# Where the first folds run, and a start written out by hand, in a Fourier-transform and expert kernel

## The chip, the core and the metric

The kernel runs on one NeuronCore of a Trainium2 chip: TensorE (PE) multiplies matrices, VectorE (DVE), ScalarE (ACT) and GpSimd (POOL) work elementwise, SyncE (SP) issues most DMAs, and POOL issues those whose addresses come from data. The metric is the device time of one execution in microseconds, as the median of repeated runs.

## The reference

```python
X = np.fft.fft(x, axis=1)          # x: 8 batches, 2496 positions, 256 features, f32
X = np.fft.fft(X, axis=2)
x = X.real.reshape(19968, 256)     # tokens
logits = x @ w_gate                # 8 experts
e_idx = np.argmax(logits, axis=1)
gate_w = softmax(logits)[e_idx]
eom = 1.0 / (1.0 + np.exp(-(x @ w_output_gate)))
for e in range(8):
    mask = e_idx == e
    h = np.maximum(x[mask] @ w1[e], 0.0)        # 256 -> 1024
    out[mask] = gate_w[mask] * eom[mask, e] * (h @ w2[e])
```

## The kernel before

**Stages.** A batch of the transform is loaded as five tiles `xt` of 128 features by 8 groups of 128 positions (512 KB each), written (batch, chunk) below. For each tile `fold1` adds the two halves (one instruction on 500 or 512 elements per partition; from batch `LB` = 3 on, two more on 250 or 256), and `fold2` forms sums and differences in two to four more instructions and stores them in `ft`. Then `dstage` multiplies by the table of the first transform on PE (f32), `devac` takes the result out of PSUM as two f16 parts `ahi` (ACT) and `alo` (DVE), scaled by a power of two that `energy`, `energy_sum` and `scale` work out of the batch's energy; `sstage` multiplies by the tables of the second transform (`tst0`, `tstm`, `tstr`, `tstq`), and `sevac` makes rows of tokens. There are five S stages a batch, so 40 steps `n` = 5 b + i. `gating(b)` picks the expert of each token and a place in the scratch `scr`, and 20 scatters a batch, indirect DMAs of POOL (L653), write the rows there.

**The experts.** After step `FSTART` = 15 the expert loop begins: `load_x_` reads rows of one expert back from `scr` by a transposing DMA (L1075), after the table `slots_a` says where they lie, and `mm1` and `mm2` (L1115, L1135) run on them. The first table needs the rows of batches 0 and 1, that is their 40 scatters. The other steps of the transform are woven into the expert loop.

**Order.** SP and POOL run in the order in which the program text issues (`PH1`), under `manual_schedule(engines=PH1)`. The order on PE, DVE and ACT is chosen by a planner from its own simulated times. `steps()` issues step by step: the D stages of the next batch, the S stage of this one, the folds of tiles further ahead (`fc` counts them; `AHEAD` bounds how far), the evacuation, pieces of the gating with five scatters each, and the squares of the expert weights on ACT (`wsquare`, L367), for which `wload` issues two 1 MB loads ahead. Seven buffers hold `xt` tiles; `load_x` issues the next load on SP when a fold is through with a tile. PSUM holds three results of D or S stages.

**Lines that the change touches.** `fold1` (L413, L416, L417): its engine is handed over by the caller; in `start` it alternates between DVE and POOL, in `steps` (L978) it is POOL except for chunk 1 of batches below 3. `fold2` (L429, L432): on POOL for chunks 2 and 4 of batches 0 and 1, else on DVE; L441 and L443 are always on DVE. `start` (L932 to L955) issues batch 0; on SP it issues the loads of all seven `xt` buffers first, and `tst0` after all folds of batch 0.

Of the kernel before, what the change touches and what calls it, by code (L numbers as in the profile page):

```python
# [19 lines left out]
KC = 5  # L20
# [210 lines left out]
def fft_moe_kernel(ctx: ExitStack, tc: tile.TileContext, xl, wg, w1, w2, tde, tdo, gt, ts0, tsm, tsr, tsq, cst, tid, out):  # L231
    nc = tc.nc
# [43 lines left out]
    if True:  # L276
# [45 lines left out]
        load_x()  # L322
# [96 lines left out]
        def fold2(b, c):  # L419
# [4 lines left out]
            W = slice(0, KW[c])  # L424
            ft = f[c] = pf.tile([128, 2, 2, 128], F32, name="ft", tag="ft", bufs=7)
            h = int(b >= LB)
            v = xts[b, c].rearrange("p (h a b) n -> p h a b n", h=2, a=2)[:, h]
            eng = nc.gpsimd if b < 2 and c in (2, 4) else nc.vector
            eng.tensor_sub(ft[:, :, 1, W], v[:, :, 0, W], v[:, :, 1, W])  # L429
            yield  # L430
            e = v[:, :, 0]
            eng.tensor_add(e[:, :, W], e[:, :, W], v[:, :, 1, W])  # L432
# [499 lines left out]
        def start():  # L932
            gt_ = gate_tables()
            next(gt_)
            for c in range(KC):
                fold1(0, c, nc.gpsimd if c % 2 else nc.vector)
                if c == 2:
                    for _ in gt_:
                        pass
                weave(fold2(0, c))  # L940
                if c > 2:
                    dstage(0, c - 3)
            for j in range(2):
                load_t(j)
            nc.sync.dma_start(tidt, tid)
            for k in range(2):
                nc.sync.dma_start(scr[DUM + 128 * k:DUM + 128 * (k + 1), :], ztile)
            energy(0)
            energy_sum(0)
            scale(0)  # L950
            smalls.clear()
            for c in range(KC):
                if c > 1:
                    dstage(0, c)
                devac(0, c)  # L955

        def steps():
            wk = 0
            fc = KC
            for n in range(5 * NB):  # L960
# [11 lines left out]
                for j in range(2, 6) if n == 0 else ():  # L972
                    load_t(j)
                while fc <= min(KC * (b + 1) + AHEAD[b >= BA][i], KC + 3 * n + 2):
                    m = fc
                    fc += 1
                    if m < NB * KC:
                        fold1(*divmod(m, KC), nc.vector if m % KC == 1 and m // KC < 3 else nc.gpsimd)  # L978
                    if m - 1 < NB * KC and m > KC:
                        fillers.append(fold2(*divmod(m - 1, KC)))  # L980
                        if n < 2:
                            weave(fillers.pop())
# [246 lines left out]

    with tc.manual_schedule(engines=PH1):  # L1230
        start()
# [62 lines left out]
```

## Time and profile before

| | us |
|---|---|
| median of the runs shown | 1174.66 |
| the runs | 1174.36, 1174.66, 2767.52 |
| profiled execution, whole | 1159.36 |
| its span, first to last instruction | 1157.5 |

The profiled execution is 15.3 us shorter than the median. A time in the trace counts from the span's start. In a row of the timeline stand the start, the duration, the engine, the line, the operation, what it writes and reads, how many instructions are merged, and in brackets the idle time before it with what ended it. "SPq" is an issue on SP's queue.

### The profile page before, as it was taken

What the parts mean: (1) busy time and instruction counts of PE and PEld (TensorE: products, weight loads), DVE (VectorE), ACT (ScalarE), POOL (GpSimd) and SP (SyncE); (2) the same over time, 40 slices, a digit from 0 to 9 for tenths busy, and PEclk for the clock granted to TensorE, in tenths of its full rate; (3) what the DMA queues carried; (4) which work ended last, traced back from release to release, by engine and by line L of the source; (5) the groups of instructions that cost most, each with busy time, mean ns of one, the idle gap of its engine ahead of it and who ended that gap; (6) DMA issues with size and microseconds to landing.
All of it is one profiled execution on the core that took longest, in us unless ns stands there. A gap on an engine that the chain in (4) does not pass through costs nothing.

```text
span 1157.5 us, 28573 instructions
## 1 busy us (share of the span) xinstructions
PE 1052.7 (91%) x10060; PEld 934.4 (81%) x10060; DVE 833.0 (72%) x1535; ACT 731.6 (63%) x1216; POOL 498.6 (43%) x430
## 2 busy tenths in 40 slices
PE   3877469989999999998999999999999989999998
PEld 3666458878788887887878888889989979998887
DVE  7876797878988747568445454588777867787684
ACT  2598657666666654553445454587777767777684
POOL 5418873786577444462564122223222322322231
PEclk9998779999999999999999999999999999999999
DMA  7778554755547545464767524557457464655651
GB/s 285 300 260 346 214 161 137 222 164 149 168 144 183 138 131 151 137 166 143 186 182 177 142 57 122 154 159 196 128 170 201 125 166 113 175 166 147 183 130 30
DMA packets 158213, 194.09 MB, mean 168 GB/s; under 512 B 117885, under 2 KB 118527, under 8 KB 156020
## 3 DMA queue, kind: packets, MB, share of 16 engines
q1 hardware_dynamic: 142100, 149.68, 46.6%
q0 software_dynamic: 15824, 42.14, 10.9%
q8 instruction: 79, 1.29, 0.5%
q14 instruction: 66, 0.54, 0.2%
q10 hardware_dynamic: 144, 0.44, 0.1%
HBM read 193.47 MB, written 43.46 MB: 205 GB/s over the span
## 4 chain that ended last, share of the span: by engine, by line
PE 63%; DVE 11%; issue 8%; POOL 6%; ACT 5%; DMA 3%; SPq 2%; another core or an unknown queue 0%; POOLq 0%; DVEq 0%; ACTq 0%
PE hp L1115 30%; PE yp L1135 29%; PE psb_t L521 3%; POOL scr L653 2%; POOL out_dram L1143 2%; DVE w1b L1096 1%; DVE rt L549 1%; DMA raw1b<-in_w_dram 1%; DVE hl L1120 1%; POOL xt L413 1%; SPq L1057 1%; ACT wt L367 1%; DVE w0b L1096 1%; DVE xt L432 1%; ACT w1b L1095 1%
## 5 line engine op out<-in xcount | busy, mean ns | idle before, releaser
L1115 PE MATMUL hp<-xr,w0b 128*128 128x256 f16 (+2 forms) x4224 | 482.8, 264 | 20.9 <-DVE hl L1120 13.7
L1135 PE MATMUL yp<-w1b,hh 128*128 128x256 f16 x2608 | 450.4, 273 | 6.7 <-issue 3.6
L1143 POOL DMA_INDIRECT out_dram<-y,xf x163 | 214.7, 1317 | 554.1 <-ACT y L1142 520.2
L1115 PEld LDWEIGHTS <-w0b 128*128 128x128 f16 x4224 | 384.6, 98 | 70.4 <-issue 15.4
L1135 PE MATMUL yp<-w1b,hl 128*128 128x256 f16 (+3 forms) x1304 | 356.0, 273 | 2.0 <-issue 2.0
L1135 PEld LDWEIGHTS <-hh 128*128 128x128 f16 x2608 | 251.9, 98 | 40.3 <-issue 11.9
L1119 ACT ACTIVATE hh<-hp 128x512 f16<-128x512 f32 (+4 forms) x352 | 194.0, 554 | 131.6 <-PE hp L1115 112.9
L1120 DVE SCALAR_TENSOR_TENSOR hl<-hp,hh 128x512 f16<-128x512 f32 (+4 forms) x352 | 222.0, 637 | 68.2 <-ACT hh L1119 56.9
L1096 DVE SCALAR_TENSOR_TENSOR w1b<-raw1b,ssc,w1b 128x1024 f16<-128x1024 f32 x144 | 186.3, 1294 | 111.7 <-ACT w1b L1095 90.3
L1096 DVE SCALAR_TENSOR_TENSOR w0b<-raw0b,ssc,w0b 128x1024 f16<-128x1024 f32 x144 | 190.2, 1324 | 69.6 <-ACT w0b L1095 51.7
L653 POOL DMA_INDIRECT scr<-rows,desti x160 | 178.6, 1116 | 73.3 <-issue 43.8
L1095 ACT ACTIVATE w0b<-raw0b,ssc 128x1024 f16<-128x1024 f32 x144 | 164.6, 1146 | 64.6 <-PE hp L1115 28.6
L1095 ACT ACTIVATE w1b<-raw1b,ssc 128x1024 f16<-128x1024 f32 x144 | 165.2, 1148 | 55.0 <-PE yp L1135 25.0
L1135 PEld LDWEIGHTS <-hl 128*128 128x128 f16 (+3 forms) x1304 | 127.9, 98 | 19.0 <-issue 4.2
L1142 ACT ACTIVATE y<-yp,ysc 128x256 f32<-128x256 f32 (+1 forms) x163 | 68.9, 470 | 43.4 <-PE yp L1135 34.2
L413 POOL TENSOR_TENSOR xt<-xt 128x500 f32<-128x500 f32 (+1 forms) x35 | 47.0, 1346 | 21.8 <-DMA xt<-in_xl_dram 19.5
L482 PE MATMUL psb_t<-tdet,ft 128*125 128x290 f32 (+1 forms) x120 | 36.2, 458 | 16.5 <-DVE alo L495 12.2
L482 PEld LDWEIGHTS psb_t<-tdet,ft 128*125 128x125 f32 (+1 forms) x120 | 24.7, 213 | 25.1 <-issue 13.5
L521 PE MATMUL psb_t<-ahi,tstq 125*128 125x145 f16 (+1 forms) x384 | 41.4, 227 | 3.3 <-DVE rt L539 2.0
L521 PEld LDWEIGHTS <-tstq 125*128 125x128 f16 (+1 forms) x576 | 38.6, 97 | 5.4 <-issue 4.6
L551 ACT CAST rows<-rt 128x516 f16<-128x516 f32 x40 | 25.0, 625 | 21.7 <-DVE rt L549 11.3
L484 PE MATMUL psb_t<-tdet,ft 128*125 128x145 f32 (+1 forms) x100 | 22.9, 313 | 16.8 <-DVE alo L495 9.4
(214 smaller groups left out, 916.4 us busy)
## 6 DMA issues: line engine op xcount, KB each, us to landing
raw0b<-in_w_dram SPq DMA_DIRECT2D x144, 512.0 KB
raw1b<-in_w_dram SPq DMA_DIRECT2D x144, 512.0 KB
xt<-in_xl_dram SPq DMA_DIRECT2D x40, 512.0 KB
wt<-in_w_dram SPq DMA_DIRECT2D x16, 1024.0 KB
out_dram<-y,xf POOLq DMA_INDIRECT x163
scr<-rows,desti POOLq DMA_INDIRECT x160
xr<-scr SPq DMA_TRANSPOSE x88
xf<-scr SPq DMA_DIRECT2D x75, 2.0 KB
```

The lines of the kernel that those rows point to most:

```text
L413: eng.tensor_tensor(x0, x0, x1, op=ALU.add)
L482: nc.tensor.matmul(o[:, 0:290], ft[:, k, par, W], tdab[:, k], start=(k == 0), stop=(k == 1))
L521: nc.tensor.matmul(ps[:, k, c0:c0 + 145], tab[hl][t][K], a[K, kc, par, c0:c0 + 145], start=(n == 0), stop=(n == len(terms) - 1))
L653: free_order("scr", batch=b, inst=nc.gpsimd.indirect_dma_start(out=scr[:, :], out_offset=bass.IndirectOffsetOnAxis(ap=desti[:, j:j + 1], a ...
L1095: nc.scalar.activation(w[:, 0], r, AF.Copy, scale=sc)
L1096: nc.vector.scalar_tensor_tensor(w[:, 1], r, sc, w[:, 0], op0=ALU.mult, op1=ALU.subtract)
L1115: nc.tensor.matmul(ps[:, k, T], w1v[:, hl, kc, (f % 4) * 128:(f % 4 + 1) * 128], a["x"][:, x, T], start=(m == 0), stop=(m == 5))
L1119: nc.scalar.activation(hh[:, G, T], ps[:, :, T], AF.Relu)
L1120: nc.vector.scalar_tensor_tensor(hl[:, G, T], ps[:, :, T], 0.0, hh[:, G, T], op0=ALU.max, op1=ALU.subtract)
L1135: nc.tensor.matmul(a["yp"][0:M, u], a[k, h][:, f, u * 128:u * 128 + M], w2v[:, hl, f], start=(g == 0 and f == 0 and m == 0), stop=(h == 1 ...
L1142: nc.scalar.activation(a["y"][0:M, u], a["yp"][0:M, u], AF.Copy, scale=ys[0:M, u:u + 1])
L1143: free_order("out", nc.gpsimd.indirect_dma_start(out=out[:, :], out_offset=bass.IndirectOffsetOnAxis(ap=a["f"].bitcast(I32)[0:M, u, 1:2], ...
```

## The change

The program text of `start` is now the order on every engine: it stands in a `manual_schedule()` of its own, ahead of the one for `PH1`. In it, all folds of batch 0 run on DVE; the energy and its scale are issued before the folds of chunk 4 are through; two D stages stand between the folds, and each of the last two behind an evacuation; chunk (1, 0) gets its `fold1` there. SP issues the five tiles of batch 0, then one part of `tst0`, one tile of batch 1, the other part, one more tile; `tstm` and `tstr` after the first folds have freed tiles, and `tstq` behind these.

In `steps`, `fold1` of batches 1, 2 and 3 runs on DVE, and of batches 4 to 7 still on POOL. `fold2` is on DVE for all. The counter starts at `KC + 1`, since (1, 0) is folded.

```diff
-        load_x()
+        load_x(KC - 1)
...
-            eng = nc.gpsimd if b < 2 and c in (2, 4) else nc.vector
-            eng.tensor_sub(ft[:, :, 1, W], v[:, :, 0, W], v[:, :, 1, W])
+            nc.vector.tensor_sub(ft[:, :, 1, W], v[:, :, 0, W], v[:, :, 1, W])
...
         def start():
             gt_ = gate_tables()
-            next(gt_)
-            for c in range(KC):
-                fold1(0, c, nc.gpsimd if c % 2 else nc.vector)
-                if c == 2:
-                    for _ in gt_:
-                        pass
-                weave(fold2(0, c))
-                if c > 2:
-                    dstage(0, c - 3)
             for j in range(2):
                 load_t(j)
+                load_x(1)
+            def fold(c):
+                weave(fold2(0, c))
+            fold1(0, 0, nc.vector)
+            next(gt_)
+            fold(0)
+            fold1(0, 1, nc.vector)
+            for _ in gt_:
+                pass
+            fold(1)
+            for c in range(2):
+                dstage(0, c)
+            fold1(0, 2, nc.vector)
+            fold(2)
+            fold1(0, 3, nc.vector)
+            fold(3)
+            fold1(0, 4, nc.vector)
+            energy(0)
+            energy_sum(0)
+            dstage(0, 2)
+            for j in range(2, 4):
+                load_t(j)
+            fold(4)
             nc.sync.dma_start(tidt, tid)
...
-            energy(0)
-            energy_sum(0)
+            for j in range(4, 6):
+                load_t(j)
             scale(0)
             smalls.clear()
             for c in range(KC):
-                if c > 1:
-                    dstage(0, c)
                 devac(0, c)
+                if c < 2:
+                    dstage(0, c + 3)
+                if c == 2:
+                    fold1(1, 0, nc.vector)
...
-            fc = KC
+            fc = KC + 1
...
-                for j in range(2, 6) if n == 0 else ():
-                    load_t(j)
...
-                        fold1(*divmod(m, KC), nc.vector if m % KC == 1 and m // KC < 3 else nc.gpsimd)
+                        fold1(*divmod(m, KC), nc.vector if m // KC < 4 else nc.gpsimd)
...
+    with tc.manual_schedule():
+        start()
     with tc.manual_schedule(engines=PH1):
-        start()
```

## Rows read from the trace of the kernel before

**Rows 1.** The stretches of the span: instructions' busy time by engine, the granted clock of TensorE (PEclk), the busy share of the DMA engines, and GB/s; first five stretches of the whole, then the one in which POOL waits for its first scatter.

```profile
10.00:80.00 70.00, 48.10 (x394) 39.02 (x394) 64.18 (x142) 43.72 (x99) 29.36 (x27) 0.93 0.73 275
80.00:120.00 40.00, 26.80 (x234) 23.17 (x234) 25.27 (x75) 31.78 (x62) 33.22 (x32) 0.82 0.91 347
120.00:158.00 38.00, 21.22 (x186) 20.28 (x187) 32.13 (x105) 22.37 (x47) 31.18 (x31) 0.77 0.45 155
178.00:640.00 462.00, 431.49 (x4125) 382.34 (x4125) 324.94 (x706) 262.17 (x467) 258.28 (x226) 0.99 0.59 162
640.00:1157.50 517.50, 507.63 (x4962) 452.86 (x4959) 368.11 (x470) 354.05 (x514) 135.57 (x99) 1.00 0.53 142
...
54.00:80.69 26.69, 18.93 (x210) 16.53 (x210) 23.60 (x75) 25.93 (x56) 0.39 (x1) 1.00 0.57 215
```

**Rows 2.** The chain that ended last, in order of time, around the last scatter of batch 1 and the first load of the experts' rows: start, duration, what.

```profile
155.44 2.49 DMA scr<-rows,desti
...
157.98 1.35 SPq L1075
```

**Rows 3.** POOL's own timeline from its first scatter to the first one of batch 1.

```profile
80.69 1.14 POOL L653 DMA_INDIRECT scr<-rows,desti  x1 [26.30 <-ACT qs L537]
...
86.98 1.27 POOL L413 TENSOR_TENSOR xt<-xt 128x500 f32<-128x500 f32 x1
...
89.87 1.17 POOL L653 DMA_INDIRECT scr<-rows,desti  x1 [0.15 <-issue]
...
96.36 1.28 POOL L413 TENSOR_TENSOR xt<-xt 128x512 f32<-128x512 f32 x1
...
99.63 1.17 POOL L653 DMA_INDIRECT scr<-rows,desti  x1 [0.15 <-issue]
...
113.34 0.97 POOL L653 DMA_INDIRECT scr<-rows,desti  x1 [0.30 <-issue]
114.33 1.27 POOL L413 TENSOR_TENSOR xt<-xt 128x500 f32<-128x500 f32 x1
...
121.11 1.00 POOL L653 DMA_INDIRECT scr<-rows,desti  x1 [1.34 <-issue]
```

**Rows 4.** The timeline of all engines at the start, from the last energy of batch 0 to the first S stage.

```profile
13.91 0.19 ACT L410 ACTIVATION_READ_ACCUMULATOR sq<-xt 128x1 f32 x1
...
19.45 0.28 PE L460 MATMUL psm_t<-es,cs 128*128 128x1 f32 x2
...
28.99 0.15 DVE L270 TENSOR_SCALAR p_x<-psm_t 128x1 int32<-128x1 int32 x1
...
29.42 1.38 ACT L494 ACTIVATE ahi<-psb_t,p_x 125x580 f16<-125x580 f32 x2 [0.47 <-DVE p_x L272]
...
36.62 0.23 PE L521 MATMUL psb_t<-ahi,tst 125*128 125x145 f16 x1
...
38.64 1.25 POOL L413 TENSOR_TENSOR xt<-xt 128x500 f32<-128x500 f32 x1 [9.86 <-DMA xt<-in_xl_dram]
...
38.78 1.39 DVE L441 TENSOR_TENSOR ft<-xt 128x250 f32<-128x250 f32 x1
```

**Rows 5.** DVE's groups from 8 us to 60 us, shapes apart: count, busy us and mean ns of one, then the idle time before them.

```profile
L432 DVE TENSOR_TENSOR xt<-xt 128x250 f32<-128x250 f32 x11 | 7.4, 678 | 0.1
...
L429 DVE TENSOR_TENSOR ft<-xt 128x250 f32<-128x250 f32 x11 | 6.0, 554 | 1.2 <-issue 1.2
L441 DVE TENSOR_TENSOR ft<-xt 128x250 f32<-128x250 f32 x6 | 5.1, 844 | 0.1
L443 DVE TENSOR_TENSOR ft<-xt 128x250 f32<-128x250 f32 x6 | 4.6, 759 | 0.0
L549 DVE TENSOR_TENSOR rt<-eo 128x258 f32<-128x258 f32 x4 | 3.8, 988 | 0.0
L413 DVE TENSOR_TENSOR xt<-xt 128x500 f32<-128x500 f32 x4 | 3.7, 936 | 2.4 <-ACT sq L410 2.4
...
L413 DVE TENSOR_TENSOR xt<-xt 128x512 f32<-128x512 f32 x1 | 1.7, 1727 | 0.0
```

**Rows 6.** The same lines of DVE from 200 us to 1100 us, and one `fold1` on DVE at 33 us, when POOL was idle.

```profile
L549 DVE TENSOR_TENSOR rt<-eo 128x258 f32<-128x258 f32 x34 | 13.4, 434 | 0.2
...
L432 DVE TENSOR_TENSOR xt<-xt 128x250 f32<-128x250 f32 x10 | 4.1, 412 | 0.1
...
33.05 0.67 DVE L413 TENSOR_TENSOR xt<-xt 128x500 f32<-128x500 f32 x1
```

**Rows 7.** POOL's folds from 0 to 60 us by line: count, busy us, mean ns, idle before.

```profile
L413 POOL TENSOR_TENSOR xt<-xt 128x500 f32<-128x500 f32 (+1 forms) x13 | 18.1, 1407 | 21.5 <-DMA xt<-in_xl_dram 19.5 <-DVE alo L495 1.9
...
L429 POOL TENSOR_TENSOR ft<-xt 128x250 f32<-128x250 f32 (+1 forms) x4 | 3.4, 841 | 1.8 <-DVE xt L413 1.1 <-DVE es L456 0.6
...
L417 POOL TENSOR_TENSOR xt<-xt 128x250 f32<-128x250 f32 x3 | 2.5, 834 | 0.0
```

**Rows 8.** DVE's timeline where batch 1's gating ends and where the first table is made.

```profile
117.08 1.44 DVE L429 TENSOR_TENSOR ft<-xt 128x250 f32<-128x250 f32 x1 [4.61 <-POOL xt L417]
...
118.64 0.50 DVE L626 TENSOR_TENSOR desti<-r_dest,cs 128x20 int32<-128x20 f32 x1
...
149.58 0.69 DVE L552 TENSOR_TENSOR rows<-rt,rows 128x516 f16<-128x516 f32 x1
...
153.53 0.10 DVE L765 SCALAR_TENSOR_TENSOR slots_a<-cs,r_rwa 128x12 int32<-128x12 f32 x1
```

More of the change, by code (lines that the diff above doesn't have):

```diff
@@ L427, in fold2 @@
             v = xts[b, c].rearrange("p (h a b) n -> p h a b n", h=2, a=2)[:, h]
-            eng = nc.gpsimd if b < 2 and c in (2, 4) else nc.vector
-            eng.tensor_sub(ft[:, :, 1, W], v[:, :, 0, W], v[:, :, 1, W])
+            nc.vector.tensor_sub(ft[:, :, 1, W], v[:, :, 0, W], v[:, :, 1, W])
             yield
             e = v[:, :, 0]
-            eng.tensor_add(e[:, :, W], e[:, :, W], v[:, :, 1, W])
+            nc.vector.tensor_add(e[:, :, W], e[:, :, W], v[:, :, 1, W])
             if c in (0, 2):
```

## The prediction

> **What bounds the kernel now.** I read the stretches first. From 178 us on PE is busy 431.5 of 462 us and then 507.6 of 517.5 us [rows 1]: the expert part is a stream of matmuls, and a fold on another engine can save little there. Before it, PE is busy 48.1 of 70, 26.8 of 40 and 21.2 of 38 us, at a granted clock of 0.93, 0.82 and 0.77 of the full 2.4 GHz. So the change is worth what it takes off the time at which the experts can start, and no more.
>
> What sets that start is in the chain of waits: the last scatter of batch 1 is issued at 155.44 and needs 2.49 us to land, and the first transposing load goes out at 157.98 [rows 2]. Behind that scatter lies POOL's own line: it idles 26.30 us until 80.69, and from there the 40 scatters of batches 0 and 1 and seven folds follow each other almost without a hole [rows 3]. The reader should see three pieces: when the first scatter can go (80.69), how long POOL takes to its 20th (113.34), and when batch 1's scatters may start (121.11). The first piece is bound by VectorE and ScalarE: from 10 to 80 us DVE is busy 64.2 of 70 us, and from 54 to 80.69 ACT 25.9 of 26.7 us [rows 1].
>
> **Part 1, the start by hand.** PE has the energy of batch 0 at 19.45 us, and DVE reads it at 28.99: the planner had put folds of batch 1 ahead of it. The first `ahi` comes at 29.42 and the first S stage at 36.62 [rows 4]. By hand, DVE does for batch 0 five `fold1` of 0.67, ten instructions of 0.41 (two a chunk), four more of 0.41 for the pairs and two of half the size, about 0.28 by halving with a fixed part (an estimate from 0.41): 9.65 us [rows 6]. The squares on ACT, which must read a tile before its fold, end at 14.1 [rows 4]; that leaves the last chunk after them, so the folds end near 19 and the energy's matmul, behind two D stages, near 19.9. The three scale instructions give `ahi` at about 20.5. That is a head start of 29.4 - 20.5 = 8.9 us for the first S stage.
>
> The tables do not hold it up: five tiles, two more and `tst0` are about 6 MB, and at the 275 GB/s of the first stretch (a mean that contains idle time) [rows 1] they take 22 us, so they are there by about 24, before the S stage needs them near 28. The price of the order is that DVE waits between 23 and 29 for D stages 3 and 4, which need PSUM buffers back, with only one fold of batch 1 put there; batch 1's folds, which before were under way by 23 us, now stand behind the last `alo`.
>
> **Part 2, the folds on DVE.** Until 60 us POOL does 13 `fold1`, four L429 and as many L432, and three L416 and L417 each [rows 7]. On DVE at undisturbed durations these cost 13 x 0.67 + 8 x 0.41 + 6 x 0.41 = 14.5 us. What DVE gets back is read from the same lines with and without POOL at work [rows 5, 6]: L432 11 x (0.678 - 0.412) = 2.9; L429 11 x (0.554 - 0.41) = 1.6; L441 and L443 6 x (0.844 - 0.41) + 6 x (0.759 - 0.41) = 4.7; L549 4 x (0.988 - 0.434) = 2.2; L413 4 x (0.936 - 0.67) + (1.727 - 0.67) = 2.1. Together 13.5 us. One case seen closely: POOL adds from 38.64 to 39.89, and an L441 that starts beside it takes 1.39 instead of 0.41 us and ends 0.28 after POOL [rows 4]. So the move costs DVE net 14.5 - 13.5 = +1.0 us until 60 us.
>
> The Trainium skill, "SBUF — State Buffer", section "Who interferes with whom", says that a VectorE instruction with two SBUF inputs and a GpSimd instruction that reads SBUF exclude each other, and the later one blocks fully. The L441 of rows 4 agrees; if all of POOL's 29.4 us of folds had blocked DVE, DVE would gain 14.9 us net, and the sum below would be larger. I go by the rows, since POOL is the one that waits where it came second.
>
> **The first scatter.** It comes earlier by at most the head start, 8.9 us, if nothing else of DVE stands before batch 0's gating; and by -1.0 us, so later, if all of DVE's work stands before it as now. In between, the three batch-3 folds (3,0) to (3,2), 3 x (0.67 + 2 x 0.41) = 4.5 us, belong to steps 5 to 7 and can be done after batch 0's evacuations. I take 4.5 - 1.0 = 3.5 us earlier: 77.2. It is nearer to the DVE bound because DVE is at 92% there.
>
> **POOL's line.** Two folds leave it between the first and the 20th scatter: (3,3) occupies 86.98 to 89.87 and (3,4) 96.36 to 99.63, less the 0.30 us between any two scatters: 2.6 + 3.0 = 5.6 us [rows 3]. DVE takes them over for 2 x 1.5 us in a stretch where it is busy 25.3 of 40 us [rows 1], and its own wait for them goes. Batch 4's folds stay on POOL, between the 20th scatter and batch 1's first. So (4,0) starts at 114.33 - 3.5 - 5.6 = 105.2, and POOL is free for batch 1 after (4,0) and (4,1), which last until 119.77 (121.11 less 1.34 idle), at 110.7.
>
> Is batch 1 ready then? Before, its `desti` came at 118.64, but DVE had stood 4.61 us for POOL's (4,0) with `desti` queued behind [rows 8]; with that stall gone and the 3.5 us, it comes at 118.64 - 4.61 - 3.5 = 110.5. Both agree: batch 1's scatters start at 110.7 instead of 121.11, **10.4 us earlier**. Their own line, 20 scatters and batch 4's other three folds, is not changed. The last scatter then goes at 145.0, and the experts' load at 147.6.
>
> The other input of that load is `slots_a`, ready at 153.53, 4.4 us before it was used, after the row L552 at 149.58 of step 15 has freed a buffer [rows 8]. It has to move by more than 6.0 us with the rest. It depends on the same DVE and ACT work and loses the same stall, so I let it.
>
> **Sum.** 1159.36 - 10.4 = 1149 for an execution like the profiled one. The median of runs stands 15.3 us above it; I take the difference as belonging to the way of running, so 1174.66 - 10.4 = **1164**. In the expert part the planner orders anew; nothing in the diff adds work there, and I put that at zero, with 5 us to each side as an estimate, of the size of single holes of PE in the 30 us that it idles from 178 to 640 us [rows 1].
>
> **Rivals.**
> *The table, not the scatter.* If `slots_a` does not move, the load moves only by its slack of 4.4 us: 1170; with nothing gained at all 1175. For it: DVE is busy 32.1 of 38 us from 120 to 158 [rows 1], and the folds of batch 4 on POOL still disturb it. Against: the steps before it lose the stall.
> *DVE becomes the bound, and the kernel slower.* The 14.5 us of moved work come onto an engine that is busy 92%. If what POOL's folds cost DVE does not come back, because other waits fill the place, the first scatter is later by 14.5 us and POOL gives back 5.6: 1174.66 + 8.9 = 1184. With R us coming back the sum of the parts is R - 14.5 + 4.5 + 5.6 + 1.3 = R - 3.1 (the 1.3 is POOL's idle before batch 1): it decides from R under 3.1, or under 7.6 if the batch-3 folds are not put off, where I count 13.5. Against it is the L441 of rows 4. The Trainium skill, "Perfetto Trace Analysis", section "Optimizing Scalar/DVE Operations", says that when DVE is saturated, moving work off it, even to GpSimd, may help; this change does the reverse. The same place says that the shared read port may undo such a move, which is what rows 5 and 6 show.
> *More.* If the whole 8.9 us head start passes, the first scatter is at 71.8 and the sum 8.9 + 5.6 + the 1.3 us of idle before batch 1 = 15.8, so 1159; with a good order of the expert part another 5 to 8, about 1152.
>
> **How the numbers follow.** The forecast has 0.55 (its own range 1157 to 1169), the table rival or no change 0.20 (1169 to 1177), slower 0.12 (1177 to 1190), more 0.13 (1146 to 1157). The range 1151 to 1178 leaves out the ends of the last two. Two per cent, about what a measurement of this kernel can tell from no change, is 23.5 us: below 1151 or above 1198. The whole stretch before the experts offers 15.8, so faster needs another 8 us from the expert part: 0.13, with what I may have overlooked there. Slower by so much needs the slower rival and a bad order together: 0.05. Within 2%: 0.82.
>
> **What would show it.** In the profile after: the first L495 near 21 to 22 us and the first L521 near 28 instead of 36.6; no POOL fold before 80 us; L432, L441 and L443 near 0.41 us before 60 us; the first scatter near 77; 20 scatters in a row without a fold, 28 us (113.34 + 0.97 - 80.69 - 5.6); batch 1's first scatter near 111; the first L1075 near 147.6; and after it the rest of the span as long as before, about 999.5 us. I am wrong if DVE's folds of batch 1 push batch 0's S stages back so that the first scatter stays at 80 (part 1 worth nothing), if `slots_a` comes last, or if the span after the first L1075 changes by more than 5 us.

## The result, and the profile after

The changed kernel takes 1177.17 us (median of 20 runs) against 1171.41 us of the kernel before beside it: ratio 1.0053, 95% interval 1.0035 to 1.0072. The forecast was 1164 on a kernel before of 1174.66, a ratio of 0.991. The profiled execution takes 1177.51 us, its span 1175.6. That of the kernel before (1159.36) is shorter than all of the kernel's runs here (1165.67 and more), so the two profiles differ by more than the medians do. In the changed kernel the scatter is L652, the second folds are L428, L431, L440 and L442, the S matmul is L520 and the first transposing load L1091.

The stretches, as in [rows 1], and one more from 90 to 108 us:

```profile
10.00:80.00 70.00, 50.97 (x397) 41.43 (x398) 64.61 (x186) 51.53 (x110) 1.13 (x1) 0.95 0.89 344
80.00:120.00 40.00, 26.33 (x231) 21.77 (x229) 19.29 (x50) 24.30 (x49) 24.90 (x25) 0.74 0.68 241
120.00:158.00 38.00, 20.21 (x179) 19.29 (x178) 32.01 (x117) 22.49 (x49) 27.54 (x27) 0.78 0.37 134
178.00:640.00 462.00, 419.80 (x3999) 369.76 (x3998) 327.47 (x701) 259.16 (x462) 250.25 (x222) 0.98 0.58 156
...
90.00:108.00 18.00, 4.65 (x24) 2.01 (x23) 3.05 (x6) 4.83 (x9) 14.43 (x16) 0.57 0.70 253
```

Up to 80 us it goes nearly as forecast: DVE has taken the folds over and is busy 64.61 us where it was 64.18. From 90 to 108 us TensorE does 4.65 us of work in 18. DVE's groups from 8 to 60 us, as in [rows 5]:

```profile
L413 DVE TENSOR_TENSOR xt<-xt 128x500 f32<-128x500 f32 x16 | 10.8, 675 | 4.5 <-ACT sq L410 4.3
...
L431 DVE TENSOR_TENSOR xt<-xt 128x250 f32<-128x250 f32 x14 | 5.7, 417 | 0.2
...
L440 DVE TENSOR_TENSOR ft<-xt 128x250 f32<-128x250 f32 x6 | 2.5, 416 | 0.1
```

The second folds take 0.417 and 0.416 us. POOL's timeline, as in [rows 3]:

```profile
78.84 1.13 POOL L652 DMA_INDIRECT scr<-rows,desti  x1 [77.62 <-ACT ahi L493]
...
104.25 0.98 POOL L652 DMA_INDIRECT scr<-rows,desti  x1 [0.30 <-issue]
105.32 1.26 POOL L413 TENSOR_TENSOR xt<-xt 128x500 f32<-128x500 f32 x1
...
125.46 1.01 POOL L652 DMA_INDIRECT scr<-rows,desti  x1 [14.55 <-ACT rows L550]
```

Twenty scatters stand in a row, and (4,0) starts at 105.32. Then POOL, which was to be the bound, stands idle for 14.55 us. What came late is TensorE; the waits of all engines from 80 to 126 us (engine, what it made, what it waited for: us in total, times, longest):

```profile
PEld L520 <- issue: 16.9, 17, 2.0
POOL scr L652 <- ACT rows L550: 14.5, 1, 14.5
...
PE psb_t L520 <- issue: 13.7, 16, 1.8
DVE eo L544 <- ACT qb L542: 11.3, 1, 11.3
```

"issue" is time for which the profile names nothing. TensorE's timeline of the same stretch:

```profile
97.21 0.28 PE L520 MATMUL psb_t<-ahi,tstq 128*128 128x145 f16 x1 [0.43 <-issue]
99.34 0.28 PE L520 MATMUL psb_t<-alo,tstq 128*128 128x145 f16 x1 [1.84 <-issue]
100.75 0.28 PE L520 MATMUL psb_t<-ahi,tstq 128*128 128x145 f16 x1 [1.13 <-issue]
101.47 0.28 PE L520 MATMUL psb_t<-ahi,tst 125*128 125x145 f16 x1 [0.43 <-issue]
103.56 0.28 PE L520 MATMUL psb_t<-alo,tst 125*128 125x145 f16 x1 [1.82 <-issue]
...
108.04 0.45 PE L520 MATMUL psb_t<-ahi,tst 125*128 125x145 f16 x2
```

The matmuls, singly or two together, start about 0.71 us apart or a multiple of it (100.75 to 101.47; 101.47 to 103.56), where they otherwise follow each other at 0.06 to 0.13 us. The granted clock is 0.50 (1.2 GHz) from 92.7 us until past its end, TensorE having been mostly idle before it fell. The slow stretch ends at 107.9, 3.7 us after the 20th scatter started. DVE stands 11.28 us for ACT's part of the S stage's evacuation, whose input TensorE makes, and batch 1's gating, its `desti` (124.51), its scatters and the first load (162.76; before 157.98 [rows 2]) come later for it.

### The profile page after: what moved, and what is told of

Read it like the earlier page. It is cut to its first block, busy times and chain, and to the rows that moved or that the text cites. A ratio compares the mean times of both kernels' runs of the same rounds, so it can differ in the third digit from the quotient of the medians.

```text
span 1175.6 us, 28547 instructions
## 1 busy us (share of the span) xinstructions
PE 1059.3 (90%) x10060; PEld 937.1 (80%) x10060; DVE 834.1 (71%) x1568; ACT 730.3 (62%) x1216; POOL 459.0 (39%) x397
## 4 chain that ended last, share of the span: by engine, by line
PE 56%; issue 12%; DVE 9%; POOL 8%; ACT 7%; DMA 3%; another core or an unknown queue 3%; SPq 2%; POOLq 0%; ACTq 0%; DVEq 0%
PE hp L1131 27%; PE yp L1151 26%; POOL scr L652 4%; PE psb_t L520 3%; POOL out_dram L1159 2%; ACT wt L367 2%; DVE w1b L1112 2%; POOL xt L413 1%; DVE hl L1136 1%; ACT w1b L1111 1%; DMA raw1b<-in_w_dram 1%; DVE w0b L1112 1%; DMA wt<-in_w_dram 1%; SPq L1073 1%
## 5 line engine op out<-in xcount | busy, mean ns | idle before, releaser
L1136 DVE SCALAR_TENSOR_TENSOR hl<-hp,hh 128x512 f16<-128x512 f32 (+4 forms) x352 | 222.3, 637 | 79.9 <-ACT hh L1135 73.9
L652 POOL DMA_INDIRECT scr<-rows,desti x160 | 173.8, 1086 | 140.1 <-ACT ahi L493 77.6
L520 PEld LDWEIGHTS <-tstq 125*128 125x128 f16 (+1 forms) x576 | 39.2, 97 | 16.2 <-issue 13.6
L520 PE MATMUL psb_t<-ahi,tstq 125*128 125x145 f16 (+1 forms) x384 | 43.4, 228 | 8.9 <-issue 6.0
L481 PE MATMUL psb_t<-tdet,ft 128*125 128x290 f32 (+1 forms) x120 | 34.9, 444 | 11.6 <-DVE lsc L465 3.9
L520 PEld LDWEIGHTS <-tst 128*128 128x128 f16 (+1 forms) x384 | 31.6, 111 | 16.8 <-issue 15.7
L544 DVE SCALAR_TENSOR_TENSOR eo<-psb_t,qb 128x290 f32<-128x290 f32 x64 | 26.2, 450 | 22.2 <-ACT qb L542 19.5
L520 PE MATMUL psb_t<-alo,tstq 125*128 125x145 f16 (+1 forms) x192 | 38.2, 225 | 3.5 <-issue 3.4
L520 PE MATMUL psb_t<-ahi,tst 125*128 125x145 f16 (+1 forms) x256 | 35.1, 253 | 6.0 <-issue 4.8
```

The costliest lines, as they stand in the source:

```text
L481: nc.tensor.matmul(o[:, 0:290], ft[:, k, par, W], tdab[:, k], start=(k == 0), stop=(k == 1))
L520: nc.tensor.matmul(ps[:, k, c0:c0 + 145], tab[hl][t][K], a[K, kc, par, c0:c0 + 145], start=(n == 0), stop=(n == len(terms) - 1))
L544: nc.vector.scalar_tensor_tensor(eo[:, k], ps[:HN, 0, 0:290], 2.0 ** -SH, qb, op0=ALU.mult, op1=op)
L652: free_order("scr", batch=b, inst=nc.gpsimd.indirect_dma_start(out=scr[:, :], out_offset=bass.IndirectOffsetOnAxis(ap=desti[:, j:j + 1], a ...
L1136: nc.vector.scalar_tensor_tensor(hl[:, G, T], ps[:, :, T], 0.0, hh[:, G, T], op0=ALU.max, op1=ALU.subtract)
```

## The experiments

Runs of a group were made on one chip, one after the other, and share runs of the kernel before. Its own median moved between groups, which matters below: 1171 us in the measurement above ("first" in the table), 1161 in the group after it, and 1135, 1133, 1134 and 1134 in the four later ones; one and the same chip gave 1161 and, later, 1135. I call the four later ones quiet (the expectations also say session or call for a group). "1st", "20th", "21st" and "40th" are the starts of scatters, `desti` is that of batch 1, "load" the first transposing load, "401st" the start of the 401st matmul of the experts' first product (the expectations give the 400th, 0.1 to 0.2 us earlier); ratios are against the kernel before of the group, as on record, and are not quite the quotients of the two medians (1125.83 / 1133.13 is 0.9936 for the 0.9922 below). The times in the table are of one profiled execution each. Most are within 3 us of their kernel's median; the quiet one of the kernel before is not (1141.56 for 1134.04), nor is that of two folds back (1144.27 for 1139.37).

| group | kernel | 1st | 20th | desti | 21st | 40th | load | 401st | ratio (95%) |
|---|---|---|---|---|---|---|---|---|---|
| first | before | 80.7 | 113.3 | 118.6 | 121.1 | 155.4 | 158.0 | 298.9 | |
| | changed | 78.8 | 104.2 | 124.5 | 125.5 | 160.2 | 162.8 | 305.5 | 1.0053 (1.0035 to 1.0072) |
| 1161 | before | 83.1 | 116.0 | 121.3 | 123.8 | 158.3 | 160.8 | 303.4 | 0.9989 (0.9964 to 1.0015) |
| | changed | 77.9 | 102.9 | 123.0 | 124.0 | 159.7 | 162.8 | 303.7 | 1.0019 (0.9998 to 1.0040) |
| | start only | 80.1 | 111.0 | 117.0 | 118.7 | 152.1 | 154.9 | 302.6 | 0.9998 (0.9977 to 1.0019) |
| | folds only | 81.4 | 106.1 | 127.5 | 131.1 | 166.3 | 169.2 | 311.4 | 1.0066 (1.0044 to 1.0088) |
| 1135 | two folds back | 78.3 | 110.1 | 118.0 | 121.2 | 157.3 | 160.0 | 307.0 | 1.0032 (1.0018 to 1.0047) |
| | pauses | 79.1 | 110.5 | 106.5 | 117.2 | 152.9 | 155.4 | 297.0 | 0.9974 (0.9958 to 0.9990) |
| | before, two folds moved | 88.8 | 114.7 | 114.5 | 123.4 | 157.9 | 160.3 | 300.9 | 1.0008 (0.9988 to 1.0028) |
| | quarter of the weights | 84.5 | 111.6 | 124.0 | 125.0 | 160.4 | 163.0 | 303.3 | one run |
| 1133 | changed | 77.6 | 104.1 | 116.7 | 117.7 | 153.9 | 156.5 | 292.6 | 0.9959 (0.9943 to 0.9974) |
| | folds only | 81.7 | 106.9 | 117.6 | 121.2 | 156.4 | 159.3 | 299.6 | 1.0024 (1.0006 to 1.0042) |
| | start only | 79.6 | 111.3 | 109.5 | 118.6 | 153.2 | 155.6 | 291.2 | 0.9922 (0.9903 to 0.9941) |
| | two more on DVE | 85.0 | 110.8 | 115.9 | 116.8 | 151.3 | 153.8 | 294.5 | 0.9970 (0.9953 to 0.9986) |
| 1134 | before | 84.4 | 117.3 | 122.6 | 125.0 | 159.3 | 161.8 | 303.9 | one run |
| | later folds | 79.1 | 105.4 | 108.5 | 109.5 | 147.6 | 150.3 | 292.5 | 0.9952 (0.9937 to 0.9967) |
| | start, later folds | 79.4 | 111.0 | 109.3 | 112.3 | 149.0 | 151.6 | 294.7 | 0.9997 (0.9986 to 1.0009) |
| 1134 | later folds, late load | 79.2 | 105.7 | 108.8 | 109.8 | 153.5 | 155.9 | 298.7 | 1.0007 (0.9988 to 1.0025) |
| | later folds | 78.3 | 104.8 | 107.7 | 108.7 | 146.9 | 149.5 | 292.3 | 0.9946 (0.9928 to 0.9965) |
| | start only | 79.9 | 111.2 | 108.5 | 118.0 | 152.5 | 155.0 | 291.0 | 0.9918 (0.9888 to 0.9948) |

**Each part alone** (the group at 1161). Both kernels unaltered, then the start by hand with batches 1 to 3 folded where they were, all but (1, 0), then the start of before with the folds moved.

> The kernel before once more, unchanged, for a second profile. In the profile of the changed kernel TensorE executes its instructions one by one, about 0.71 us apart, from 90 to 107.9 us of the span, waiting for nothing that the trace shows; the first profile of the kernel before has no such stretch, but its execution (1159.36 us) is 12 us shorter than the median of its 20 runs (1171.41). Theory A, slow issue is part of most executions of both kernels: this profile shows such a stretch too, and takes about 1170. Theory B, the change brought it on: no such stretch, and a profiled time like 1159 to 1171 without it.

> The changed kernel once more, unchanged. Theory B, the change brings the slow issue on by what it puts ahead of it: the stretch stands again near 90 to 108 us and the ratio is 1.005. Theory C, the stretch falls at random: it is absent or elsewhere in this profile, and then the first load of the experts' rows goes out near 150 us instead of 162.8.

Start only, against the changed kernel:

```diff
-            nc.vector.tensor_sub(ft[:, :, 1, W], v[:, :, 0, W], v[:, :, 1, W])
+            eng = nc.gpsimd if b == 1 and c in (2, 4) else nc.vector
+            eng.tensor_sub(ft[:, :, 1, W], v[:, :, 0, W], v[:, :, 1, W])
...
-            nc.vector.tensor_add(e[:, :, W], e[:, :, W], v[:, :, 1, W])
+            eng.tensor_add(e[:, :, W], e[:, :, W], v[:, :, 1, W])
...
-                        fold1(*divmod(m, KC), nc.vector if m // KC < 4 else nc.gpsimd)
+                        fold1(*divmod(m, KC), nc.vector if m % KC == 1 and m // KC < 3 else nc.gpsimd)
```

> Only the start by hand: batch 0 as in the change, folds of batches 1 to 3 on the engines of before. Theory B with the start as its cause (loads of expert weights and tiles issued some 12 us earlier): the slow stretch appears, ratio 1.00 to 1.01. Rival, the folds on VectorE are what slows: no slow stretch, first scatter at 76 to 78 us, ratio 0.992 to 0.998.

Folds only, against the kernel before:

```diff
-            eng = nc.gpsimd if b < 2 and c in (2, 4) else nc.vector
+            eng = nc.gpsimd if b < 1 and c in (2, 4) else nc.vector
...
-                        fold1(*divmod(m, KC), nc.vector if m % KC == 1 and m // KC < 3 else nc.gpsimd)
+                        fold1(*divmod(m, KC), nc.vector if m // KC < 4 else nc.gpsimd)
```

> Only the folds: fold1 of batches 1 to 3 and fold2 of batch 1 on VectorE, the start of before. By the prediction's sum, POOL's line is 5.6 us shorter between its first and its 20th scatter and VectorE pays about 1 us: ratio 0.994 to 0.997. Rival, VectorE is the bound: first scatter later than 80.7 us, ratio above 1.0. If the slow stretch comes with it, it is not the start that brings it on.

At this level the loss lies with the folds (1.0066), not with the start (0.9998). TensorE issues slowly again in both kernels whose 20 scatters stand in a row: from 90 to 106 us in the changed one (12.6 us of waits of the S matmuls put down to issue) and from 95 to 109 in folds only (11.6). In the kernel before there is no such stretch, in start only 5.6 us of it; there two folds of batch 3 part the scatters into 5, 5 and 10. My theory was that the unbroken run brings it.

**Is it the run of scatters?** (the group at 1135). Two folds back on POOL, against the changed kernel:

```diff
-                        fold1(*divmod(m, KC), nc.vector if m // KC < 4 else nc.gpsimd)
+                        fold1(*divmod(m, KC), nc.vector if m < 3 * KC + 3 else nc.gpsimd)
```

> The changed kernel with one thing undone: the first folds of (3,3) and (3,4) run on POOL again, between the scatters of batch 0. Theory A (an unbroken run of POOL's scatters makes TensorE's instructions come one by one, about 0.71 us apart, from the eleventh scatter or so on until they have landed): the folds break the run into 5, 5 and 10, the slow stretch from 90 to 107.9 us is gone or is under 8 us long and lies in the last ten scatters, the 20th scatter goes at 108 to 111, batch 1's first at 114 to 119 instead of 124 to 125.5, and the time is 0.990 to 0.998 of before. Theory B (the slow stretch comes from the weight and input loads at over 340 GB/s, which now run earlier): loads are the same, the stretch stays at 90 us, batch 1's first scatter at 124, ratio 1.002 to 1.006. Theory C (it is the DVE folds of batches 1 to 3 as such that bring the loss): eighteen of nineteen instructions in twenty are where they were, the ratio stays over 1.001.

Pauses in their place, against the changed kernel:

```diff
+    rest = kp.tile([128, 512], F32, name="rest")
...
+                    if b == 0 and j in (4, 9):
+                        for _ in range(5):
+                            nc.gpsimd.memset(rest, 0.0)
```

> The changed kernel with all folds of batches 1 to 3 left on DVE, and five memsets of a scratch tile (128x512 f32, some 3 us together by the size of the memset of 128x258 at 0.31 us) put on POOL after the 5th and after the 10th scatter of batch 0; nothing else. They compute nothing that is used. Theory A: a pause without any fold is enough; the slow stretch is gone or under 8 us, the 20th scatter goes at 108 to 111, batch 1's first at 113 to 118, ratio 0.988 to 0.998. Theory B: the stretch stays at 90 us and batch 1's first scatter comes at 124 to 130; ratio 1.002 to 1.010. Theory C: the same as B in time, with DVE and not PE as what is waited for.

The two folds alone moved, against the kernel before:

```diff
-                        fold1(*divmod(m, KC), nc.vector if m % KC == 1 and m // KC < 3 else nc.gpsimd)
+                        fold1(*divmod(m, KC), nc.vector if m % KC == 1 and m // KC < 3 or m in (3 * KC + 3, 3 * KC + 4) else nc.gpsimd)
```

> The kernel before with one thing changed: the first folds of (3,3) and (3,4) on DVE, so that POOL's 20 scatters of batch 0 stand in a row. Theory A: a slow stretch of TensorE appears from about 94 us (the eleventh scatter) to about 109, with waits put down to issue on the S stages of 10 to 18 us in all, batch 1's first scatter no earlier than before (121 to 131), ratio 1.002 to 1.008. Theory C, and my prediction's own step: nothing like it; the 20th scatter 5.6 us earlier (107.7), batch 1's first about 113 to 116, ratio 0.994 to 0.999.

A quarter of the weights, against the changed kernel:

```diff
-                nc.sync.dma_start(wq[k], wsrc[k % 2][k // 2])
+                nc.sync.dma_start(wq[k][:, 0:512], wsrc[k % 2][k // 2][:, 0:512])
...
-            nc.scalar.activation(wt, wt, AF.Square, accum_out=wen[:, k:k + 1])
+            nc.scalar.activation(wt[:, 512:2048].rearrange("p (a b) -> p a b", a=3), wt[:, 0:512].unsqueeze(1).broadcast_to([128, 3, 512]), AF.Square, accum_out=wen[:, k:k + 1])
```

> The changed kernel with the loads for the expert weights' energy cut to a quarter (256 KB instead of 1 MB each, sixteen of them from step 1 to 15), and the square on ACT taken over that quarter three times (1536 elements instead of 2048), so that the weights' scales come from a part of them; the rest of the kernel is as changed. It leaves the scatters in a row. Theory A: the slow stretch is still there, begins some ten scatters after the first and ends when the last has landed; batch 1's first scatter at 118 to 126. Theory B: with 12 MB less to move the DMA share falls well under 0.9 from 80 to 100 us, the stretch is gone, and batch 1's first scatter comes at 106 to 113.

The theory fell as it stood, that the run alone brings the slow issue. Two folds moved and a quarter of the weights have 20 scatters in a row, and no wait of TensorE's matmuls from 85 to 110 us is put down to issue in them. Loads alone do not bring it either: two folds moved has a DMA share of 0.98 from 90 to 106 us and 365 GB/s. What is new is the group: nowhere in these four does TensorE show 0.71 us spacing. So none of the four can tell what it takes at the 1161 level. Two folds back, expected to gain, lost; the cause of that stays open.

**The parts again, where it is quiet** (the group at 1133), with one run that takes two more folds off POOL, against the changed kernel:

```diff
-                        fold1(*divmod(m, KC), nc.vector if m // KC < 4 else nc.gpsimd)
+                        fold1(*divmod(m, KC), nc.vector if m < 4 * KC + 2 else nc.gpsimd)
```

> The changed kernel unaltered. In the four runs before this one no stretch of TensorE with instructions 0.71 us apart was seen, not even with 20 scatters in a row (the kernel before with two folds moved, and the changed kernel with a quarter of the weight loads), and the kernel before took 1135 us instead of 1161 or 1171, so my theory A (the unbroken run of scatters alone brings it) has fallen. Theory D: the slow issue is a state of the chip that holds for a session and stretches the kernel before as well (by 26 us, spread over the expert part); in a session with it the changed kernel is hit from 90 to 108 us, in one without it my prediction's steps hold. So: if the kernel before is near 1135 here, no slow stretch, 20th scatter at 103 to 105, batch 1's first at 110 to 113, last of batch 1 at 145 to 149, ratio 0.990 to 0.997. If it is at 1155 or more: slow stretch from 90, batch 1's first at 124 to 126, ratio 1.001 to 1.006. Theory E (the new order of the folds has a loss of its own, whatever the session): ratio over 1.001 with the kernel before near 1135, too.

> The start of before, with the folds of the first four batches on DVE as in the change (1.0066 in the first session). Theory D, kernel before near 1135: no slow stretch, the first scatter at 81 to 84, the 20th at 106 to 109, batch 1's first at 113 to 117, ratio 0.994 to 1.000; kernel before at 1155 or more: slow stretch from the eleventh scatter on, ratio 1.004 to 1.009. Theory E: over 1.003 in either.

> The start written out by hand, with the folds of batches 1 to 3 where they were (0.9998 in the first session). Theory D: without the slow issue the first scatter at 79 to 81, the 20th at 110 to 113, batch 1's first at 116 to 120, ratio 0.994 to 1.000; with it 0.998 to 1.002. Theory E: as in the first session, 0.998 to 1.002.

> The changed kernel with the first folds of (4,0) and (4,1), which stand between the scatters of batches 0 and 1 on POOL, on DVE too. With two folds put back on POOL or pauses in their place, DVE stood 4.1 and 5.5 us waiting for POOL's (4,0). Theory D, kernel before near 1135: batch 1's first scatter follows the end of its gating at 105 to 109, DVE's wait for POOL is gone, the last of batch 1 at 140 to 146; slots_a, 146.5 to 146.7 in those two runs, then sets the first load of rows at 146 to 152; ratio 0.985 to 0.995. Kernel before at 1155 or more: the run of scatters is longer still and so is the slow stretch; batch 1's first at 118 to 126, ratio 0.998 to 1.008.

The changed kernel gains here, but less than the start alone, and the folds alone still lose. Batch 1's first scatter again misses 110.7, without any slow issue. DVE's timeline of the changed kernel in this group:

```profile
101.32 0.32 DVE L589 TENSOR_TENSOR r_oh<-cs,r_mx 128x160 f32<-128x160 f32 x1
107.91 1.44 DVE L428 TENSOR_TENSOR ft<-xt 128x250 f32<-128x250 f32 x1 [6.27 <-POOL xt L417]
109.27 1.00 DVE L592 TENSOR_TENSOR_SCAN r_inc<-cs,r_oh 128x160 f32<-128x160 f32 x1
...
116.72 0.17 DVE L625 TENSOR_TENSOR desti<-r_dest,cs 128x20 int32<-128x20 f32 x1
```

Its second fold of (4,0) waits 6.27 us for POOL, where (4,0) stands behind the 20th scatter, and `r_inc` and `desti` of batch 1 are queued behind it. This is the stall of [rows 8]: 4.61 us then. POOL's (4,0) starts 9.2 us earlier (105.15 for 114.33), but DVE reaches its part 10.8 us earlier (101.64 for 112.47), so the wait has grown. It also stands in another place. In the kernel before, `r_inc` ran 10.4 us ahead of the waiting fold:

```profile
106.70 0.49 DVE L593 TENSOR_TENSOR_SCAN r_inc<-cs,r_oh 128x160 f32<-128x160 f32 x1
```

There `desti` followed the waiting fold by 1.6 us (117.08 to 118.64). Now the planner has the fold ahead of `r_inc`, and 8.8 us pass from it to `desti` (107.91 to 116.72). The wait is 4.6 us in the kernel before of the next group and 3.8 in folds only, behind `r_inc` in both. In start only it is gone: `desti` comes at 109.48, and the only wait of DVE for POOL ahead of it is one for (3,3):

```profile
88.82 0.42 DVE L429 TENSOR_TENSOR ft<-xt 128x250 f32<-128x250 f32 x1 [3.01 <-POOL xt L417]
109.48 0.17 DVE L626 TENSOR_TENSOR desti<-r_dest,cs 128x20 int32<-128x20 f32 x1
```

What batch 1 waits for there is POOL, which does (4,0) and (4,1) from 112.78 until its 21st scatter at 118.58. Two more on DVE has no such wait, but its order on DVE changes from the start (first scatter at 85.0, not 77.6): its load goes 2.7 us earlier than in the changed kernel, its 401st matmul starts 1.9 us later.

**The wait alone** (the group at 1134). After the kernel before comes "later folds", against the changed kernel: it leaves DVE's order as it is up to `r_inc` and puts the folds of (4,0) to (4,2) later in the program, on DVE behind batch 1's `desti`, on POOL behind batch 1's first five scatters. "Start, later folds" makes the same edit in start only:

```diff
-                while fc <= min(KC * (b + 1) + AHEAD[b >= BA][i], KC + 3 * n + 2):
+                while fc <= min(KC * (b + 1) + AHEAD[b >= BA][i], KC + 3 * n + 2) - (11 < n < 16):
...
-                    if m < NB * KC:
+                    if m == 21:
+                        fold1(4, 0, nc.gpsimd)
+                    if m < NB * KC and m != 20:
...
```

> The kernel before, unaltered, for its profile where the chip is quiet. If the whole is near 1133: no waits of TensorE put down to issue in the expert part, first scatter at 80 to 84, 20th at 112 to 116, batch 1's first at 119 to 124, the last at 154 to 158, busy time of TensorE from 178 to 640 us 447 to 450 instead of 431.5. If it is near 1160: as in the profile of before.

> The changed kernel, with the first and second fold of (4,0) to (4,2) one to two steps later in the program, so that on DVE the second fold of (4,0) stands behind batch 1's desti instead of ahead of its r_inc, and on POOL (4,0) and (4,1) stand behind the first five scatters of batch 1; DVE's order up to r_inc is that of the changed kernel. Theory F (DVE's wait for POOL's (4,0) is what holds batch 1 up where TensorE does not issue slowly): the wait of 6.27 us is gone, desti comes at 105 to 109 instead of 116.7, batch 1's first scatter at 105.5 to 110 instead of 117.7, the last at 143 to 149 instead of 153.9, the first load of rows at 146 to 152 (slots_a at 140 to 147 may set it), ratio 0.984 to 0.993. Rival G (the moved folds cost DVE elsewhere, and the order of the expert part decides): batch 1's first scatter moves, the last scatter and the time do not, ratio 0.994 to 0.998. If TensorE issues slowly here: the run is 25 scatters, the stretch lasts longer, batch 1's first at 116 to 126, ratio 0.998 to 1.008.

> The start written out by hand, folds of batches 1 to 3 where they were, and the folds of (4,0) to (4,2) later as in the run before. Theory F: DVE waited 3.0 us for (4,0) in the start-only run (desti 109.5, batch 1's first 118.6 behind POOL's two folds); with both folds behind, batch 1's first scatter comes at 110 to 113, right after the 20th at 111, the last at 147 to 151, ratio 0.986 to 0.992 (0.9922 without the move). Rival G: ratio 0.991 to 0.996.

DVE's timeline of later folds:

```profile
103.86 0.49 DVE L592 TENSOR_TENSOR_SCAN r_inc<-cs,r_oh 128x160 f32<-128x160 f32 x1
...
108.54 0.17 DVE L625 TENSOR_TENSOR desti<-r_dest,cs 128x20 int32<-128x20 f32 x1
```

And POOL's, the 20th and the 21st scatter:

```profile
105.44 0.97 POOL L652 DMA_INDIRECT scr<-rows,desti  x1 [0.30 <-issue]
109.48 0.97 POOL L652 DMA_INDIRECT scr<-rows,desti  x1 [3.07 <-ACT qs L536]
```

With that one wait gone `desti` comes at 108.54 and the 21st scatter at 109.48 (forecast: 110.5 and 110.7), 25 scatters in a row do TensorE no harm, and the load goes 6 us earlier than in the changed kernel. Yet the ratio hardly moves (0.9952 against 0.9959; 1128.32 us on 1134.04, so 5.7 us are gained where the forecast has 10.4): theory F holds for the scatter and fails for the time. In start only the same move brings the load 4 us earlier and loses 0.75 points. The 3.0 us that its expectation takes for a wait for (4,0) are the wait for (3,3) shown above; what the move takes away there is POOL's two folds ahead of the 21st scatter (112.3 for 118.6).

**Does the load set the end?** (the last group). The pause stands ahead of the last scatter of batch 1, so it delays that, and what POOL does behind it, against later folds:

```diff
...
-                    scatter(j)
+                    scatter(j); [nc.gpsimd.memset(rest, 0.0) for _ in range(10) if b == 1 and j == 18]
```

> The changed kernel with the later folds of batch 4, and ten memsets of a scratch tile (0.57 us each by the earlier pauses, 5.7 us together) on POOL ahead of the last scatter of batch 1, which compute nothing that is used; of TensorE's 19346 rows 31 stand elsewhere, of DVE's 1498 three. Prediction's step (the experts' start sets the end, us for us): first load at 155 to 157 instead of 150.3, ratio 0.5 points above the kernel without the pause, so near 1.000. Rival H (the load has slack of its own: the woven transform work, not the start, sets the pace until the second table): load later by 5 to 6 us, 400th hp at 292 to 294, ratio within 0.15 points of the kernel without the pause, so 0.994 to 0.997.

> The changed kernel with the later folds of batch 4, unaltered, as what the run before is compared with: ratio 0.9952 as it was, 0.994 to 0.9965; first load near 150, 400th hp near 292.5. If TensorE issues slowly here, 0.998 or more, and the run of 25 scatters shows it from 90 us.

> The start by hand alone, unaltered (0.9998 in the first four runs, 0.9922 in a later call): 0.991 to 0.994 if quiet, and faster than the kernel with the later folds though its experts start 6 us later, which speaks for rival H; near 1.000 if TensorE issues slowly.

With the order of the engines nearly kept, 6.4 us at the load are 6.4 at the experts' first matmul and at the 401st, and 6.6 at the end (1134.71 against 1128.15). So rival H falls: the load has no slack. That the load alone does it is not quite shown, since DVE's next wait for a fold on POOL grows with the pause, too (9.18 us for 3.66).

What is lost between orders lies between the experts' first matmul and the 401st: 134.9 us in later folds (157.4 to 292.3), 127.3 in start only (163.7 to 291.0). All engines and then the transform's matmuls alone, in later folds:

```profile
157.43:292.31 134.88, 125.24 (x1234) 112.22 (x1235) 115.64 (x226) 91.18 (x162) 92.04 (x76) 0.96 0.61 172
157.43:292.31 134.88, 38.48 (x456) 11.87 (x96) 15.18 (x28) 11.05 (x21) 0.96 0.61 172
```

The same in start only:

```profile
163.67:290.95 127.28, 117.49 (x1163) 105.46 (x1161) 110.80 (x217) 87.56 (x158) 85.25 (x73) 0.99 0.64 177
163.67:290.95 127.28, 32.86 (x385) 10.34 (x84) 13.67 (x26) 9.17 (x19) 0.99 0.64 177
```

TensorE is busy 7.8 us longer in later folds and idle as long (9.6 and 9.8 us), so the 7.6 us are work and not a wait: 71 matmuls more of the transform take 5.6 us of them, and the granted clock is a little lower (0.96 for 0.99). Start only has done these matmuls ahead of the experts' first one, while it waited for the load. By the 401st matmul both have done the same on TensorE (some 2064 matmuls), and what the earlier load brought was to start the experts with less of the transform done.

## Why the prediction was wrong

**Right:** the first `alo` (22.3, forecast 21 to 22), the first S stage (27.3, forecast near 28), the folds' price on DVE (L431 and L440 at 0.417 and 0.416 us; that DVE is busy only 0.4 us more until 80 us says little by itself, in a stretch where it is busy 92%), the first scatter (78.8, 77.9 and 77.6 in three profiles, forecast 77.2; against the kernel before at the same level 1.9, 5.2 and 6.8 us earlier, forecast 3.5), and that a later load of the experts' rows comes out whole at the end (late load). The table rival did not come: in every profile the load follows the 40th scatter by 2.5 to 3.0 us. (4,0) started at 105.3, forecast 105.2, in part by luck: 7.2 us came off POOL's line ahead of it, not 5.6, and the first scatter was 1.6 us later than forecast. The Trainium skill, "SBUF — State Buffer", section "Who interferes with whom", says that DVE and POOL exclude each other at the ports they share; the traces agree: no POOL fold stands there now and DVE's take 0.41, and the L428 at 107.91 above, beside a fold of POOL (107.83 for 1.24 us), takes 1.44.

**The step that failed** is "Is batch 1 ready then?". It took `desti` as 118.64 - 4.61 - 3.5 = 110.5, "with that stall gone". The stall was not gone: (4,0) stays on POOL behind the scatters, and the planner put DVE's part of it ahead of `r_inc`, where before it stood behind. Where it is quiet, the term -4.61 is +1.66 (6.27 us), and `desti` comes at 116.7; with the term made true, at 108.5. Moving the folds away from POOL did not take that one away.

Where it is not quiet, a second assumption of that step failed: that TensorE keeps its pace while POOL scatters. It was idle for 13.4 of the 18 us from 90 to 108, `desti` came at 124.5 and the load at 162.8 instead of 147.6. Up to the 401st matmul TensorE stood idle 75.0 us in the kernel before and 75.6 in the changed one in the first measurement, 73.4 and 73.8 at 1161, but 75.9 and 67.4 where it is quiet (the 75.9 in the profile that is 7.5 us over its median): what the change saves there is gone where TensorE issues slowly. None of the rivals had TensorE come late; "DVE becomes the bound", the slower one, was not it, since DVE is busy 19.3 of 40 us there.

**"So the change is worth what it takes off the time at which the experts can start"** failed too, and with it the rest put at zero. It held for a delay in a given order (late load), not between orders: with the load at 150.3 (later folds), 2.7 us after the forecast, 5.7 us were gained and not 7.7. In quiet groups the first 400 matmuls of the experts' first product took between 127.0 us (changed) and 139.1 (two folds back): it depends on how much of the transform is left to be done among them and on how long TensorE idles. That spread is larger than everything that the two parts moved. The prediction's own sign of being wrong, a span after the load that changes by more than 5 us, came in the first profile (1012.9 us for 999.5), though not in the second of the same kernel (997.3). And the 15.3 us between profile and median, which the sum took over as belonging to the way of running, are not there in the changed kernel (1177.51 and 1177.17).

**What each part is worth,** where it is quiet: the start -0.8 points (0.9922 and 0.9918), the folds +0.2 (1.0024); both together 0.9959. The start alone has the lowest median of all that was run, 1125.83 against 1133.13 us, and is faster than both kernels; at 1161 it was level (0.9998).

## What to carry to other kernels

Before a stall is booked as gone, look which instruction it waits for and whether that one moves, and what will stand behind it in the new order: here the work that was moved to DVE was not the work DVE waited for, and moving the rest only made DVE come earlier and wait longer. With a planner that orders engines anew, a gain at one milestone has to be followed to the next (here the 401st matmul). Where the bound engine can do its other work while it waits, an earlier start gains only the idle time that it takes away, so compare idle time up to a point at which both kernels have done the same work. Delaying a milestone with the order kept shows what it is worth; look what else the delay moved. Run the kernel before beside every experiment: its own time moved by 38 us, where each part was worth 3 to 9.

## What the runs showed of the hardware

TensorE can fall to one instruction each 0.71 us or a multiple, with no engine named, and the granted clock then falls to 0.50. In three profiles with 20 indirect DMAs in a row at a level of 1161 or more it began at the ninth to eleventh of them and lasted until 3 to 4 us after the last had started; with such a run at 1133 to 1135 it was not there in eight profiles. So the run alone does not bring it, nor the level alone: at 1161 the two kernels whose run is broken show 5.6 us of it or next to none (0.2). That it takes both is what these profiles suggest; no run varied the run of scatters alone at the high level.

What the level is stays open. It shows in the experts' part: from the 401st to the 1201st matmul of the first product there are 241 to 254 us in the six profiles of the first two groups and 225.9 to 226.4 in the 14 quiet ones. The experts' matmuls, and DVE's scaling of one weight, from 200 to 1100 us in the kernel before, first profile:

```profile
L1115 PE MATMUL hp<-xr,w0b 128*128 128x256 f16 (+3 forms) x3820 | 441.6, 265 | 20.4 <-DVE hl L1120 13.1 <-issue 3.3 <-DVE p_x L270 1.9
L1135 PE MATMUL yp<-w1b,hh 128*128 128x256 f16 (+1 forms) x2382 | 411.6, 273 | 6.7 <-issue 3.6 <-ACT y L1142 1.4 <-DVE w1b L1096 1.1
L1096 DVE SCALAR_TENSOR_TENSOR w0b<-raw0b,ssc,w0b 128x1024 f16<-128x1024 f32 x129 | 169.9, 1320 | 66.7 <-ACT w0b L1095 48.9 <-issue 17.7
```

The same in the quiet profile of the kernel before:

```profile
L1115 PE MATMUL hp<-xr,w0b 128*128 128x256 f16 (+2 forms) x3939 | 453.5, 265 | 14.8 <-DVE hl L1120 12.1 <-DVE p_x L270 1.9 <-DVE es L456 0.5
L1135 PE MATMUL yp<-w1b,hh 128*128 128x256 f16 (+1 forms) x2448 | 420.2, 273 | 2.9 <-ACT y L1142 1.7 <-DVE w1b L1096 1.1
L1096 DVE SCALAR_TENSOR_TENSOR w0b<-raw0b,ssc,w0b 128x1024 f16<-128x1024 f32 x134 | 177.9, 1331 | 60.0 <-ACT w0b L1095 57.6 <-DMA xf<-scr 2.2
```

The waits for issue are there in the first and gone in the second, and not on TensorE alone: DVE has 39.7 us of them in that stretch of the first profile, 17.7 in the line shown, the longest 4.8, and none in the second. So the higher level is no matter of one engine. The Trainium skill, "Runtime: NRT & Kernel Launch", section "Instruction fetch mechanics", says that an engine's instructions are fetched in blocks of 16 KB while the last ones run, and that this is mostly hidden. From 85 to 108 us of the changed kernel one packet of that size was moved, 0.3% of 16 engines' 23 us, about 1.1 us, so the trace doesn't show the fetch as what was slow; no run here tells what was.
